# Routed attention and two expert layers on one Trainium2 core: first and last expert swapped, SyncE's order and one queue changed

## The chip, the cores and the metric

The kernel runs on 1 core of a Trainium2 chip. The metric is the device time of one execution in microseconds (us). The engines are TensorE (PE; its weight loads are listed apart as PEld), VectorE (DVE), ScalarE (ACT), GpSimd (POOL) and SyncE (SP), which issues most of the transfers. "Lnnn" is a line of the kernel before.

## The reference, cut to what matters

Three stages follow each other; batch 2, sequence 768.

```python
# 1. attention, 8 heads of 64; only keys of the query's cluster (16 clusters) count
mask = q_assign[:, :, :, None] == k_assign[:, :, None, :]
scores = np.where(mask, scale * q @ k.T, -1e9)
x = softmax(scores) @ v                      # -> x[2, 768, 512]
# 2. one of 8 experts per token
e = fresh_e if (s == 0 or local_gate[b, s] < 0.5) else prev_e
h = np.maximum(x[b, s] @ w1[e], 0.0)         # 512 -> 1024
out[b, s] = p[e] * (h @ w2[e])               # 1024 -> 512
# 3. gated projection, K = 5 taps of a causal convolution
gate = sigmoid(sum(conv_w[k] * shifted(x, k) for k in range(5)))
y = (gate * (x @ w_val)) @ w_out
```

For the inputs that are timed, the experts 0, 1 and 2 get 54, 88 and 118 tokens of the first batch and 88, 65 and 62 of the second; expert 3 gets 170 in all, and the others, by falling number, 289, 228, 211 and 163.

## The kernel before

**Attention.** Sixteen (batch, head) problems are worked as 8 pairs, 12 items of 128 queries each. `prep_steps(g)` prepares a pair while the pair ahead of it is worked. Its steps `stack1` and `stack2` are transfers from SBUF to SBUF; `stack2` (L455) brings the one-hot rows of the clusters into `st`, which PE reads at L668. SyncE issues them in program order with the other loads.

**Routing.** After each half batch, tokens are scattered by expert into `xslots` in HBM by GpSimd, a slot of 428 rows for each of 8 experts and for 3 more: an expert of `HALVED` has a slot for each batch. `keep_rows(gq)` (L513) also copies the rows of a half batch from `xnat` to `xall`; for the last one it is an entry of the list `work`.

**Experts.** They are worked in 8 positions. `AT` gives the expert of the positions 0, 1, 6 and 7; positions 2 to 5 take the experts 4 to 7 in falling order of tokens. `CAPS` is the number of rows worked in each position, `ROWS` the rows of the two batches of a halved expert. The first batch of position 0's expert is worked ahead, in `early_load`, `early_rows` and `early_products`. `do_mm1(k)` is the first product: weights stand, `CAPS[k]` columns of tokens move; experts of `WHOLE` use plain float32 weights (each product two matmul instructions), others split weights (`whi`, `wlo`) and split rows (`xhi`, `xlo`) in three terms. `do_mm2(k)` is the second product: tokens stand, 512 columns of weights move, 24 matmuls for a block of rows; where `FOLD[k]` holds, the last block of 64 rows holds its high and low parts side by side and needs 16, and its two halves are added after (L1206, L1207). Positions 6 and 7 are worked by halves at the end (`do_half`): the first batch of both, then the second batch of both; in between the first batch's rows are loaded back from `x2d` (L1330) for stage 3.

**Rows and weights.** `do_x(k, part)` transposes the rows of a position into one PSUM buffer `xp` (`ps_x` has one) and copies them out; it is called inside `do_mm1(k - 1)`, in two parts for position 2, which has 300 rows. Weights of 1 MB come in through SyncE in the order of `worder`; those to be split go through three staging buffers (`wstg`, `wstg1`, `wstg2`) by `w_stage(at)`, which loads the next pending block into the buffer it is given; after the second half of a split, the buffer just split is given to the next block (L1040). Block 6 is the first staged, block 7 the second.

**Order.** The order of all work is that of the program, on each engine. `tick()` runs inside the products: each tick does one entry of `work` (splits), two of `late`, and one step of `conv` once `XS["ready"]` is set. `conv` is a list of 66 steps that turn the two double-precision matrices of stage 3 into float32 pairs in 8 chunks, over a buffer `wspace` that takes the place of `xnat`: load (L260), four steps on VectorE (`b01` to `b6`), one on ScalarE, three operations on GpSimd (L269, L270, L273), store (L276, L277). What is left of `conv` is done after the first halves (L1324), ahead of the reload.

**End.** Stage 3 ends with `project_out`: ScalarE copies a tile of 128 rows from PSUM to `os_`, a pool of two buffers, and SyncE stores it.

Of the kernel before, what the change touches and what calls it, by code (L numbers as in the profile page):

```python
# [8 lines left out]
F32 = mybir.dt.float32  # L9
# [10 lines left out]
NQT = 6  # L20
NC_ = 16
E = 8
CAPS = (128, 176, 300, 240, 224, 176, 192, 192)
WHOLE = (0, 1, 5, 6, 7)
PACK = 64
AT = {0: 0, 1: 3, E - 2: 2, E - 1: 1}
HALVED = (0, 1, 2)
ROWS = {0: (128, 128), 1: (96, 96), 2: (128, 64)}
V = E + len(HALVED)
NF = len(AT)  # L30
NS = E - NF
SLOT = 428
# [9 lines left out]
def routed_attention_moe_kernel(  # L42
# [12 lines left out]
    nc = tc.nc  # L55
# [8 lines left out]
    xslots = dram.tile([V * SLOT + NCH * 128, XC], F32, name="xslots")  # L64
# [97 lines left out]
    for n, k in enumerate(free):  # L162
        nc.gpsimd.memset(capk[:, :, n], float(CAPS[k]))

# [167 lines left out]
    def w_stage(at):  # L332
        if pending:
            j = pending.pop(0)
            home[j] = at
            wraw[j] = at.tile([128, 2048], F32, tag="w", name="wraw")
            w_load(j, wraw[j])
# [31 lines left out]
    def prep_steps(g):  # L369
        b, p = pairs[g]  # L370
        x = X[g]
        xx = xx_p.tile([128, 4, S], F32R, tag="xx", name="xx")
        st = [st_p.tile([128, 4, S], F32R, tag=f"st{h}", name=f"st{h}") for h in range(2)]
# [80 lines left out]

        def stack2(h):  # L455
            r = o["ohr"].bitcast(F32)
            nc.sync.dma_start(st[h][64:80, 2, :].bitcast(F32), r[32 + 16 * h:48 + 16 * h, :])
            nc.sync.dma_start(st[h][64:80, 3, :].bitcast(F32), r[16 * h:16 * h + 16, :])

        def S0(h, parts=None):  # L460

# [51 lines left out]
    def keep_rows(gq):  # L513
        nc.sync.dma_start(
            xall[384 * gq:384 * gq + 384, :].rearrange("(t p) c -> p t c", p=128), xnat[:, 3 * gq:3 * gq + 3, :]
        )
# [276 lines left out]
    EA = {}  # L793

    def early_load():
        EA["xs"] = xin_p.tile([128, 2, S], F32, tag="x", name="exs")[:, 0, :XC]
        nc.sync.dma_start(EA["xs"], xslots[0:128, :])

    def early_rows():
        xs = EA["xs"]  # L800
# [22 lines left out]
    for i in range(NI):  # L823
        g, qb, t, h = items[i]
# [67 lines left out]
    h_p = mpool("hp", 1)  # L892
    WX = (max(CAPS[0::2]), max(CAPS[1::2]))
    ehh = h_p.tile([128, 8, 2 * WX[1]], F32, tag="h1", name="ehh")[:, :, :128]
# [132 lines left out]
    work = []  # L1027
# [10 lines left out]
    def queue_split(j):  # L1038
        work.append(lambda: w_split(j, 0))
        work.append(lambda: (w_split(j, 1), w_stage(home[j])))  # L1040
# [5 lines left out]
    def tick():  # L1046
# [13 lines left out]
    XT, HT, IDS, PW = {}, {}, {}, {}  # L1060
    NT = [-(-c // 128) for c in CAPS]
    FOLD = [
        ROWS[AT[k]][1] == PACK if k and AT.get(k) in HALVED else 0 < (c - 1) % 128 < PACK and n > 1
        for k, (c, n) in enumerate(zip(CAPS, NT))
    ]
    TR = [
# [1 line left out]
    ]  # L1068
    XS = {}

    def load_x(k):
        if k >= E:
            return
        n, rows = NT[k], TR[k]
        XS[k] = xs_p.tile([128, -(-WX[k % 2] // 128), XC], F32, tag=f"xs{k % 2}", name="xs")
        if k == 0:
            nc.sync.dma_start(XS[k][:, 0, :], xslots[E * SLOT:E * SLOT + 128, :])
            return
        if AT.get(k) in HALVED:
            for t, c in enumerate((AT[k], E + HALVED.index(AT[k]))):  # L1080
                nc.sync.dma_start(XS[k][:TR[k][t], t, :], xslots[c * SLOT:c * SLOT + TR[k][t], :])
            return
        if k in AT:
            src = xslots[AT[k] * SLOT:AT[k] * SLOT + CAPS[k], :]
        else:
            src = xslots[bass.ds(turn[k] * SLOT, CAPS[k]), :]
        if FOLD[k] or k == 0:
            for t, r in enumerate(rows):
                nc.sync.dma_start(XS[k][:r, t, :], src[sum(rows[:t]):sum(rows[:t]) + r, :])
        else:  # L1090
            nc.sync.dma_start(XS[k][:rows[0], :n, :], src.rearrange("(t p) c -> p t c", p=rows[0]))
# [41 lines left out]
    def do_mm1(k):  # L1133
        w = CAPS[k]
        xs = XT.pop(k)
        h = HT[k] = h_p.tile([128, 8, 2 * WX[k % 2]], F32R if k else F32, tag=f"h{k % 2}", name="h")
        c0 = w - PACK if FOLD[k] else w
        for q in range(2):
            if k in WHOLE:
                terms = [(W[k, q].rearrange("p (d f) -> p d f", d=4), xs[0])]  # L1140
            else:
                whv, wlv = [t.rearrange("p (d f) -> p d f", d=4) for t in W[k, q]]
                terms = [(whv, xs[0]), (whv, xs[1]), (wlv, xs[0])]
            for fp in range(2):
                if w > 256:
                    hps = [ps_h.tile([128, 1, 512], F32, tag="h", name="hps") for _ in range(2)]
                else:
                    hps = [ps_h.tile([128, 2, 256], F32, tag="h", name="hps")]
                for fi in range(2):
                    f = 2 * fp + fi  # L1150
                    fs = slice(128 * f, 128 * f + 128)
                    hp = hps[fi][:, 0, :w] if w > 256 else hps[0][:, fi, :w]
                    for n, (a, c) in enumerate(terms):
                        for d in range(4):
                            nc.tensor.matmul(  # L1155
                                hp, a[:, d, fs], c[:, d, :w], start=(n + d == 0), stop=(n + d == len(terms) + 2)
                            )
                m = 2 // len(hps)
                for i, hp in enumerate(hps):
                    fs = slice(4 * q + 2 * fp + m * i, 4 * q + 2 * fp + m * i + m)  # L1160
                    hhi = h[:, fs, c0:c0 + w]
                    nc.scalar.activation(hhi, hp[:, :, :w], AF.Relu)  # L1162
                    for c1, c2, at_ in ((0, c0, 0), (c0, w, c0 + w)):
                        if c1 < c2 and k:
                            nc.vector.scalar_tensor_tensor(  # L1165
                                h[:, fs, at_:at_ + c2 - c1], hp[:, :, c1:c2], 0.0, hhi[:, :, c1:c2].bitcast(F32),
                                op0=ALU.max, op1=ALU.subtract,
                            )
                pops[0] = 2 if (k, q) >= (E - 1, 0) else 1
                tick()  # L1170
                if k < E - 1 and (q, fp) in ((0, 1), (1, 0)):
                    do_x(k + 1, q)
                    if q == 0:
                        load_x(k + 2)
            if k:
                queue_w(wpos[k, q])
        if k == 0:
            queue_split(R + 3)
# [35 lines left out]
    def do_mm2(k):  # L1214
        n = NT[k]
        for t in range(n):
            if t < 2:
                YP[k, t] = ps_y.tile([128, 512], F32, tag="y", name="yp")
            else:
                YP[k, t] = ps_h.tile([128, 512], F32, tag="h", name="yp3")  # L1220
        for q in range(2):
            whv, wlv = mm2_weights(k, q)
            for t in range(n):
                mm2_part(k, t, q, whv, wlv)
                if t < 2:
                    tick()
            if k:
                queue_w(wpos[k, 2 + q])
            else:
                w_stage(stg[q])  # L1230
        HT.pop(k)
        for t in sorted(range(n), key=lambda t: (not FOLD[k] or t < n - 1, t)):
            mm2_out(k, t)

    def do_half(k, t, *apart):
        YP[k, t] = ps_y.tile([128, 512], F32, tag="y", name="yp")
        for q in range(2):
            mm2_part(k, t, q, *mm2_weights(k, q))
            tick()
        mm2_out(k, t, *apart)  # L1240
# [5 lines left out]
    for n, k in enumerate(free):  # L1246
        turn[k] = nc.sync.value_load(ordi[0:1, n:n + 1], min_val=NF, max_val=E - 1)
    w_stage(stg[2])
    queue_split(R + 2)
    ey = ps_y.tile([128, 512], F32, tag="y", name="ey")  # L1250
    for q in range(2):
# [6 lines left out]
    y = y_p.tile([128, 512], F32, tag="y", name="ysb")  # L1258
    nc.scalar.activation(y, ey, AF.Copy, scale=EA["pw"])
    scatter(x2d, EA["ids"], y, 2 * S, "rows of different tokens")  # L1260
    work += [lambda: None, lambda: None, lambda: keep_rows(3)]
    late += overflow_steps()
    do_mm1(0)
    XS["ready"] = True
    do_mm2(0)
    do_mm1(1)
    for k in range(2, E - 1):
        do_mm1(k)
# [7 lines left out]
    with tc.If(nch > 0, preferred_fallthrough_block=False):  # L1276
        with tc.For_i(0, nch, 1) as j:
# [5 lines left out]
            with tc.For_i(0, nd, 1):  # L1283
                for tt in range(12):
                    xs = xs_p.tile([128, 2, XC], F32, tag="xs0", name="xst")
                    nc.sync.dma_start(xs[:, 0, :], xall[128 * tt:128 * tt + 128, :])
                    scatter(xslots, idx1[:, tt:tt + 1], xs[:, 0, :], V * SLOT + NCH * 128)
            if True:
                xs = xs_p.tile([128, 2, XC], F32, tag="xs0", name="xsl")
# [56 lines left out]
    fl = fpool("fl", 2)  # L1346
# [122 lines left out]
    def project_out(b, t, parts=1):  # L1469
        op = OP.pop((b, t))  # L1470
        r0 = S * b + 128 * t
        os_ = fl.tile([128, 512], F32, tag="os", name="os")
        w = 512 // parts
        for n in range(parts):
            cs_ = slice(w * n, w * n + w)
            (nc.vector.tensor_copy if n else nc.scalar.copy)(os_[:, cs_], op[:, cs_])
            (nc.scalar if n else nc.sync).dma_start(out[r0:r0 + 128, cs_], os_[:, cs_])
# [108 lines left out]
```

## Time and profile before

| | us |
|---|---|
| median of the runs | 541.88 (541.17 to 542.16, 3 runs) |
| profiled execution | 539.74 |
| its span, first to last instruction | 538.1 |
| PE busy | 515.7 (96%) |
| DVE busy | 353.1 (66%) |
| ACT busy | 310.0 (58%) |
| POOL busy | 91.3 (17%) |

The mean granted clock of TensorE is 0.990. "Idle before <-X" is the time that an engine stood in front of an instruction and what ended it. The timeline gives start and duration in us, a count if instructions are merged, and the idle time in brackets; SPq and ACTq are transfers issued by SyncE and ScalarE. A matmul's duration includes its pipeline; the spacing of starts is what it costs in a row of them.

### The profile page before, as it was taken

The page shows a single profiled execution, that of the slowest core. Times are in us where ns is not written, and L with a number is a line of the kernel's source. Part 1 is how long each engine was busy: PE and PEld are TensorE (multiplying, and loading weights), DVE is VectorE, ACT ScalarE, POOL GpSimd, SP SyncE. Part 2 cuts the span into 40 slices and gives each one's busy share as a digit, 9 for nine tenths or more (in the row PEclk, how much of TensorE's full clock was granted, in tenths as well). Part 3 has the DMA queues.
Part 4 walks back from the last instruction along what each step waited for, and adds up shares of the span by engine and source line. Part 5 has one row for each costly group of instructions (what it writes and reads, how often), then busy time and mean ns, then how long its engine had stood idle before and what let it go on. Part 6 is the DMA issues. An engine that isn't in the chain of part 4 may idle for free.

```text
span 538.1 us, 8817 instructions
## 1 busy us (share of the span) xinstructions
PE 515.7 (96%) x3189; PEld 409.4 (76%) x3190; DVE 353.1 (66%) x693; ACT 310.0 (58%) x592; POOL 91.3 (17%) x106
## 2 busy tenths in 40 slices
PE   7898999999999999999999499999999999999996
PEld 3775777777677767776956498979889887899885
DVE  5684767575677877655603679986367673599960
ACT  3696868677776778675112355645334463485632
POOL 5011002020203031000310020523421344100000
PEclk9899999999999999999999889999999999999999
DMA  5876787888887866810665866795978855730023
GB/s 146 225 157 212 154 278 198 242 231 207 267 202 272 191 214 135 294 47 2 201 250 193 314 213 222 242 325 194 362 242 314 311 177 203 266 139 2 19 99 117
DMA packets 35524, 108.63 MB, mean 202 GB/s; under 512 B 4718, under 2 KB 5230, under 8 KB 30869
## 3 DMA queue, kind: packets, MB, share of 16 engines
q1 hardware_dynamic: 32341, 101.15, 60.7%
q0 software_dynamic: 2176, 6.31, 3.2%
q10 hardware_dynamic: 960, 0.58, 0.4%
q8 instruction: 26, 0.43, 0.3%
q14 instruction: 21, 0.17, 0.1%
HBM read 58.39 MB, written 29.83 MB: 164 GB/s over the span
## 4 chain that ended last, share of the span: by engine, by line
PE 41%; DMA 5%; SPq 1%; DVE 1%; ACT 1%; issue 1%; ACTq 0%; DVEq 0%
PE hps L1155 13%; PE yp L1195 4%; PE yp L1197 4%; PE yp L1196 4%; PE vp L1421 2%; PE vp L1427 2%; PE vp L1422 2%; PE op L1467 2%; PE op L1466 2%; PE op L1465 2%; DMA xall<-xnat 2%; PE yp L1192 1%; PE yp L1193 1%; DMA wraw<-in_wq_dram 1%; PE xp L1118 1%
## 5 line engine op out<-in xcount | busy, mean ns | idle before, releaser
L675 DVE TENSOR_REDUCE mx<-s 128x1 f32<-128x768 f32 x96 | 91.6, 954 | 59.5 <-PE s L668 53.4
L704 ACT COPY pt<-tp 128x384 f32<-128x384 f32 x148 | 65.7, 483 | 54.4 <-PE tp L699 54.3
L684 ACT ACTIVATE pexp<-s,mx 128x768 f32<-128x768 f32 x96 | 87.1, 907 | 6.7 <-DVE mx L675 4.5
L699 PE MATMUL tp<-ident,pexp 128*128 128x128 f32 x576 | 81.1, 277 | 0.3 <-DVE pt L702 0.2
L699 PEld LDWEIGHTS tp<-ident,pexp 128*128 128x128 f32 x576 | 68.2, 142 | 7.7 <-ACT pt L704 3.3
L366 DVE TENSOR_TENSOR wlo<-wraw,whi 128x1024 fp32r<-128x1024 f32 x40 | 52.9, 1330 | 29.6 <-ACT whi L360 29.6
L711 PE MATMUL pv<-pt,vt 128*64 128x384 f32 x360 | 67.8, 498 | 0.0
L360 ACT CAST whi<-wraw 128x1024 fp32r<-128x1024 f32 x40 | 40.7, 1046 | 31.8 <-DMA wraw<-in_wq_dram 16.8
L664 PE MATMUL s<-st 128*128 128x384 f32 x188 | 57.3, 386 | 1.5 <-ACT pexp L684 1.5
L1155 PE MATMUL hps<-xhi,wone 128*128 128x192 f32 (+2 forms) x320 | 50.7, 318 | 0.0
L668 PE MATMUL s<-st 80*128 80x384 f32 x188 | 49.0, 342 | 1.4 <-DMA st<-ohr 1.4
L1155 PEld LDWEIGHTS hps<-xhi,wone 128*128 128x128 f32 x320 | 49.0, 195 | 1.6 <-ACT xhi L1124 0.6
L664 PEld LDWEIGHTS s<-st 128*128 128x128 f32 x188 | 28.6, 191 | 17.8 <-issue 7.3
L711 PEld LDWEIGHTS pv<-pt,vt 128*64 128x64 f32 x360 | 21.9, 136 | 23.8 <-issue 23.8
L1162 ACT ACTIVATE h<-hps 128x352 fp32r<-128x352 f32 (+5 forms) x36 | 16.9, 474 | 33.8 <-PE hps L1155 33.7
L1195 PE MATMUL yp<-whi,h 128*112 128x512 f32 (+4 forms) x88 | 35.0, 397 | 0.8 <-ACT h L1162 0.8
L668 PEld LDWEIGHTS s<-st 80*128 80x128 f32 x188 | 34.4, 190 | 1.7 <-issue 1.7
L1197 PE MATMUL yp<-whi,h 128*112 128x512 f32 (+4 forms) x88 | 34.7, 394 | 0.0
L1196 PE MATMUL yp<-wlo,h 128*112 128x512 f32 (+4 forms) x88 | 34.7, 394 | 0.0
L384 POOL TENSOR_TENSOR xx<-xkq,xx 128x768 fp32r<-128x768 f32 x8 | 14.6, 1822 | 117.5 <-ACT xx L378 117.5
L1407 DVE SCALAR_TENSOR_TENSOR gt<-xf,convw_sb,gt 128x768 f32<-128x768 f32 x32 | 32.0, 1015 | 0.4
L1165 DVE SCALAR_TENSOR_TENSOR h<-hps,h 128x128 fp32r<-128x128 f32 (+7 forms) x52 | 18.4, 391 | 16.7 <-ACT h L1162 15.1
(280 smaller groups left out, 893.0 us busy)
## 6 DMA issues: line engine op xcount, KB each, us to landing
wraw<-in_wq_dram SPq DMA_DIRECT2D x20, 1024.0 KB
st<-xx SPq DMA_DIRECT2D x48, 384.0 KB
wone<-in_wq_dram SPq DMA_DIRECT2D x12, 1024.0 KB
xslots<-padrow SPq DMA_DIRECT2D x15, 771.0 KB
xkq<-in_kq_dram SPq DMA_DIRECT2D x15, 384.0 KB
wspace<-in_wd_dram SPq DMA_DIRECT2D x8, 512.0 KB
xall<-xnat SPq DMA_DIRECT2D x4, 771.0 KB
vt<-in_v_dram SPq DMA_DIRECT2D x8, 384.0 KB
```

Of the source, the lines that this page charges most:

```text
L366: nc.vector.tensor_tensor(lo[:, c], t[:, c], hi[:, c].bitcast(F32), op=ALU.subtract)
L664: nc.tensor.matmul(ps[:, n, :384], st[:, 1, q0:q0 + 128], st[:, 0, 384 * n:384 * n + 384], start=True, stop=False)
L668: nc.tensor.matmul(ps[:, n, :384], st[0:80, 2, q0:q0 + 128], st[0:80, 3, 384 * n:384 * n + 384], start=False, stop=True)
L675: nc.vector.tensor_reduce(mx, ps[:, :, :384], axis=AX.XY, op=ALU.max, negate=True)
L684: nc.scalar.activation(pt, ps[:, :, :384], AF.Exp, bias=mx[:, 0:1], accum_out=Zt[i // 6][:, t, h:h + 1])
L699: nc.tensor.transpose(tp[:, k, :], p[:, 128 * kt:128 * kt + 128], ident)
L704: nc.scalar.copy(dst, tp)
L711: nc.tensor.matmul(PVs[u][64 * h:64 * h + 64, :], Vt[g][:, kt, h, :], PT[u, h][:, kt, :], start=(kt == 0), stop=(kt == NQT - 1), skip_grou ...
L1155: nc.tensor.matmul(hp, a[:, d, fs], c[:, d, :w], start=(n + d == 0), stop=(n + d == len(terms) + 2))
L1195: nc.tensor.matmul(yp[:r], h[:, fa, hi], whv[:, f, :], start=(q == 0 and f == 0), stop=False)
L1196: nc.tensor.matmul(yp[:r], h[:, fa, hi], wlv[:, f, :], start=False, stop=False)
L1197: nc.tensor.matmul(yp[:r], h[:, fa, lo], whv[:, f, :], start=False, stop=(q == 1 and f == 3))
```

## The change

Experts 0 and 1 change places: expert 1 goes to position 0, with 72 rows of the second batch there, expert 0 to position 7 with 64 and 96 rows, of which the block of 64 (the first batch) is folded; position 6 works 184 rows for 192. `halves` and the first line of `do_half` let the folded block be either batch. The last `keep_rows` leaves the list `work` and stands right behind the first `w_stage`; two empty entries keep their place, and `XS["ready"]` is set after the second product of position 0. `stack2` of the second pair goes to ScalarE's queue. `os_` gets four buffers.

```diff
-CAPS = (128, 176, 300, 240, 224, 176, 192, 192)
+CAPS = (72, 176, 300, 240, 224, 176, 184, 160)
-AT = {0: 0, 1: 3, E - 2: 2, E - 1: 1}
+AT = {0: 1, 1: 3, E - 2: 2, E - 1: 0}
-ROWS = {0: (128, 128), 1: (96, 96), 2: (128, 64)}
+ROWS = {1: (128, 72), 2: (120, 64), 0: (64, 96)}
...
         def stack2(h):
             r = o["ohr"].bitcast(F32)
-            nc.sync.dma_start(st[h][64:80, 2, :].bitcast(F32), r[32 + 16 * h:48 + 16 * h, :])
-            nc.sync.dma_start(st[h][64:80, 3, :].bitcast(F32), r[16 * h:16 * h + 16, :])
+            q = nc.scalar if g == 1 else nc.sync
+            q.dma_start(st[h][64:80, 2, :].bitcast(F32), r[32 + 16 * h:48 + 16 * h, :])
+            q.dma_start(st[h][64:80, 3, :].bitcast(F32), r[16 * h:16 * h + 16, :])
...
-        nc.sync.dma_start(EA["xs"], xslots[0:128, :])
+        nc.sync.dma_start(EA["xs"], xslots[AT[0] * SLOT:AT[0] * SLOT + 128, :])
...
-        ROWS[AT[k]][1] == PACK if k and AT.get(k) in HALVED else 0 < (c - 1) % 128 < PACK and n > 1
+        PACK in ROWS[AT[k]] if k and AT.get(k) in HALVED else 0 < (c - 1) % 128 < PACK and n > 1
...
+    def halves(k):
+        cols = AT[k], E + HALVED.index(AT[k])
+        return cols[::-1] if ROWS[AT[k]][0] == PACK else cols
...
-            nc.sync.dma_start(XS[k][:, 0, :], xslots[E * SLOT:E * SLOT + 128, :])
+            c = E + HALVED.index(AT[0])
+            nc.sync.dma_start(XS[k][:CAPS[0], 0, :], xslots[c * SLOT:c * SLOT + CAPS[0], :])
...
-            for t, c in enumerate((AT[k], E + HALVED.index(AT[k]))):
+            for t, c in enumerate(halves(k)):
...
-    def do_half(k, t, *apart):
+    def do_half(k, b, *apart):
+        t = b ^ (ROWS[AT[k]][0] == PACK)
...
     w_stage(stg[2])
+    keep_rows(3)
+    work += [lambda: None, lambda: None]
     queue_split(R + 2)
...
-    work += [lambda: None, lambda: None, lambda: keep_rows(3)]
     late += overflow_steps()
     do_mm1(0)
+    do_mm2(0)
     XS["ready"] = True
-    do_mm2(0)
     do_mm1(1)
...
-        os_ = fl.tile([128, 512], F32, tag="os", name="os")
+        os_ = fl.tile([128, 512], F32, tag="os", name="os", bufs=4)
```

## Rows read from the trace of the kernel before

**Rows 1.** What PE waited for over the whole span: us in total, times, longest.

```profile
PE xp L1118 <- DVE xlo L1129: 6.9, 1, 6.9
...
PE s L668 <- DMA st<-ohr: 1.4, 1, 1.4
```

**Rows 2.** Timeline of PE, positions 0 and 1.

```profile
278.18 3.74 PE L1155 MATMUL hps<-xhi,wone 128*128 128x128 f32 x32
...
293.36 4.94 PE L1155 MATMUL hps<-xhi,wone 128*128 128x176 f32 x32
...
308.54 1.45 PE L1118 MATMUL xp<-ident,xs 128*128 128x128 f32 x6 [6.85 <-DVE xlo L1129]
...
313.87 0.83 PE L1155 MATMUL hps<-xhi,whi 128*128 128x300 f32 x4
```

**Rows 3.** Timeline of VectorE in position 1.

```profile
298.94 1.22 DVE L366 TENSOR_TENSOR wlo<-wraw,whi 128x1024 fp32r<-128x1024 f32 x1
...
304.58 0.43 DVE L230 TENSOR_SCALAR wspace<-wspace 128x512 int32<-128x512 int32 x1 [4.14 <-DMA wspace<-in_wd_dram]
...
307.72 0.76 DVE L1129 TENSOR_TENSOR xlo<-xp,xhi 128x600 fp32r<-128x600 f32 x1
```

**Rows 4.** Timeline of SyncE's queue, positions 0 and 1.

```profile
279.24 11.41 SPq L326 DMA_DIRECT2D wraw<-in_wq_dram  x2
...
292.68 0.58 SPq L514 DMA_DIRECT2D xall<-xnat  x1
301.00 0.36 SPq L260 DMA_DIRECT2D wspace<-in_wd_dram  x1
```

**Rows 5.** Timeline of ScalarE, first split of block 7.

```profile
295.71 1.05 ACT L360 CAST whi<-wraw 128x1024 fp32r<-128x1024 f32 x1 [5.81 <-DMA wraw<-in_wq_dram]
```

**Rows 6.** Stretches: PE, PEld, DVE, ACT, POOL busy, PE clock, DMA share, GB/s.

```profile
288.00:294.00 6.00, 6.00 (x18) 3.02 (x18) 4.07 (x22) 1.90 (x5) 0.00 (x0) 1.00 0.38 142
...
308.50:311.00 2.50, 2.46 (x10) 2.08 (x11) 2.46 (x6) 0.66 (x1) 0.00 (x0) 0.50 1.01 419
```

**Rows 7.** The chain that ended last, first products: start, us, work (224, 176, 192 columns).

```profile
364.01 5.36 PE hps L1155 x48
...
386.83 4.78 PE hps L1155 x32
...
428.87 10.41 PE hps L1155 x64
```

**Rows 8.** Timeline of PE, start of the halves and of stage 3.

```profile
440.08 0.47 PE L1195 MATMUL yp<-whi,h 128*128 128x512 f32 x1 [0.81 <-ACT h L1162]
...
460.55 1.47 PE L1377 MATMUL x2p<-ident,x2nat 128*128 128x128 f32 x12
```

**Rows 9.** Timeline of VectorE, the folded output of half (6, 1).

```profile
456.57 0.74 DVE L1207 SCALAR_TENSOR_TENSOR ysb<-part,pw,ysb 64x512 f32<-64x512 f32 x1 [8.08 <-ACT part L1206]
```

**Rows 10.** Timeline of GpSimd in the first halves.

```profile
448.98 1.29 POOL L269 TENSOR_TENSOR wspace<-wspace 128x512 f32<-128x512 f32 x1 [1.06 <-ACT wspace L265]
...
451.59 1.29 POOL L273 TENSOR_TENSOR wspace<-wspace 128x512 fp32r<-128x512 f32 x1
453.04 0.95 POOL L635 DMA_INDIRECT x2d<-ysb,ids  x1 [0.16 <-issue]
```

**Rows 11.** Timeline of SyncE's queue, the reload.

```profile
456.04 9.41 SPq L1330 DMA_DIRECT2D x2nat<-x2d  x5
```

**Rows 12.** Timeline of ScalarE, last two output tiles.

```profile
533.37 1.06 ACT L1476 COPY os<-op 128x512 f32<-128x512 f32 x2 [1.46 <-DMA out_dram<-os]
```

**Rows 13.** Timeline of PE, its last matmul.

```profile
532.86 0.39 PE L1467 MATMUL op<-whi,gl 128*128 128x512 f32 x1
```

**Rows 14.** Timeline of ScalarE: an issue at the start, an exp of the first pair.

```profile
2.10 0.62 ACTq L171 DMA_DIRECT2D cw<-in_convw_dram  x1
...
36.01 0.90 ACT L684 ACTIVATE pexp<-s,mx 128x768 f32<-128x768 f32 x1
```

**Rows 15.** Timeline of PE, scores of the first pair.

```profile
37.93 0.59 PE L664 MATMUL s<-st 128*128 128x384 f32 x2
```

## Prediction

> **What bounds the kernel now.** I read the list of what TensorE (PE) waited for first. In 538.1 us it has one long wait, 6.9 us for VectorE's `xlo`; the longest single one after it is the 1.4 us for `st<-ohr` [rows 1]. So a change is worth what it takes from that stall, from PE's instructions, or from the tail where PE is done.
>
> PE's timeline shows where the stall is. The first product of position 1 starts at 293.36; after three quarters of it PE needs its one transpose buffer `xp` for the second part of position 2's rows and gets it 6.85 us late, at 308.54; position 2 starts at 313.87 [rows 2]. VectorE's timeline shows why: it sat 4.14 us until `wspace`, the first double-precision chunk, landed at 304.5, converted a piece, and only then did `xlo` (from 307.72), which frees `xp` [rows 3]. SyncE's timeline shows why the chunk was late: it reuses the buffer `xnat`, whose copy (L514) went out at 292.68, so L260 could go only at 301.00, and every load behind it on this queue with it [rows 4]. So the order of issue, not bandwidth, makes this stall. In 308.5 to 311 PE's granted clock is 0.50 (the 1.2 of 1.2 and 2.4 GHz): the stall cost a slow restart too [rows 6].
>
> **The change, part by part.**
>
> *SyncE's new order.* Two moves. `keep_rows(3)` goes right behind the first staged load (279.24), and the conversion starts two ticks later, in position 1. The copy took at most 8.3 us, with block 7 and position 2's rows queued ahead of it [rows 4]; issued near 280 it is over by about 289, in front of the second staged load, which goes out near 290.3 as before; were it not, each us late there would shift the rest by a us.
>
> The missing `None`s move something else. Both halves of the split of staged block 7 now fall in position 0's second product, and the second half calls `w_stage`: block 9 goes into that same buffer and waits until VectorE has done the split, and SyncE waits with it. Behind it stand block 10 (1 MB), the first chunk (0.5 MB), the second, and position 3's rows. Block 7 is on ScalarE from 295.71 [rows 5]; its two halves there take 1.05 each, VectorE's low parts 1.2 each behind, with two small steps between: VectorE is done about 299.7 (it began this half at 298.94 before [rows 3]). Block 9 then goes out at 299.7 and moves data from about 301 (301.00 to 304.5 for an unqueued half megabyte [rows 3, 4] is some 2.2 us of latency and 1.3 of transfer at 419 GB/s [rows 6], part of the latency behind the last byte). Blocks 9 and 10 and the chunk are 2.6 MB: 6.3 us at 419 GB/s. The chunk is there at about 308, later than the 304.5 of before.
>
> VectorE meets that wait in another place, though: one tick pair later, behind `xlo` part 0 and in front of part 1. Part 0: VectorE is free at 299.7, has two pairs of `h` steps, six small steps and the 0.76 of `xlo`: done about 303.0. PE, which wants `xp` at 301.5 (293.36 + 32 x 0.149 + 0.9 of transposes + 16 x 0.149, spacing from [rows 7]), stands 1.5 us. Then 0.8 of transposes and 16 matmuls: position 2 starts at 306.2 and after 0.6 needs `xlo` part 1. That is the chunk (308.0), 1.1 of conversion, 0.7 of `xlo`: 309.85, a second stall of 3.1 us. Position 2 effectively starts at 309.85 - 0.6 = 309.3, against 313.87 [rows 2]: **4.6 us gained**, if neither short stall lowers the clock. Bounds: nothing of it, if the chunk comes 4.6 later; 7.7, if it is no later than before, since 306.2 is then PE's own start.
>
> After that the conversion stays two ticks late. VectorE comes to position 2 earlier by as much as PE does, with the same work ahead, so I add nothing for it; the price is at the end (below).
>
> *Swapped experts: columns.* In the chain 64 matmuls of 192 columns take 10.41 (0.163 each) and 32 of 176 take 4.78 (0.149): 0.83 ns a column [rows 7]. Position 6 loses 8 columns, position 7 loses 32, 64 matmuls each: 0.43 + 1.70 = **2.1 us**. PE is unbroken there, so it counts. Position 0 loses 56 columns, 128 to 72. By the same slope that would be 64 x 56 x 0.83 ns = 3.0 us; but 48 matmuls of 224 one-pass columns took 5.36, 0.112 each [rows 7], no less than a matmul of 128 two-pass columns (3.74 for 32, at most 0.117 [rows 2]), where one pass at half of 0.83 ns a column would give 0.093. The near rows thus show a floor near 0.112, and I take 0; bounds 0 and 3.0. Either way it isn't on the path: the stall behind it ends with a DMA. The Trainium skill (TensorE: Matmul & The Clock Gate, section "LDWEIGHTS (loading the stationary operand)") speaks against this edit: a weight load takes the number of its columns over 1.2 ns, 107 ns for 128, however few columns follow. By it, as an estimate, position 0 would save at most 64 x 5 ns = 0.3 us; the rows of 224 columns agree, no run here has 72. The smaller load of position 0's rows and its transposes are hidden the same way.
>
> *Swapped experts: the second product of position 7.* Its 64-row half is now folded: 16 matmuls for 24, 8 x 0.233 = 1.9 us off PE (88 matmuls took the 20.47 from 440.08 to 460.55 [rows 8]). The last halves are bound by the reload, though. Before: PE started them at 440.08, the reload (L1330) went out at 456.04, PE used it at 460.55 without a recorded wait [rows 1, 8, 11]. The conversion now has two more steps left: its three GpSimd operations (448.98 to 452.9) stood ahead of the scatter of half (7, 0) (453.04) [rows 10]; now they stand behind it, and the last store and the reload behind them on SyncE. Counted from the start of the halves: 40 matmuls, +9.3; a folded output needs 2.4 from PE's end to VectorE's end (half (6, 1): 64 matmuls give 455.0, VectorE ends at 457.3 [rows 9]), +11.8; scatter 1.0; three operations 3.9, +16.9; store and reload, +17.4 (before: +16.0). PE is done at +18.6 instead of +20.5, but its first three tiles are 0.79 MB: 1.9 us at 419 GB/s and 2.2 of latency after the issue, +21.5, and the third's transposes end near +22.1 (before: +21.9). The 1.9 is lost, and I take **-0.2**; bounds +1.9 and, with a reload 1.3 later still, -1.5.
>
> *Output staging, 4 buffers.* Near the end ScalarE stood 1.46 us for `out_dram<-os`, that is for a buffer, and copied the last two tiles from 533.37 one behind the other [rows 12]. PE's last matmul ends at 532.86 + 0.39 = 533.25 [rows 13]. With four buffers tile 4 is copied before that and the last copy starts near 533.4 instead of 534.05: **0.65 us**; bounds 0 and 0.8.
>
> *Second pair's one-hot rows from ScalarE.* SyncE sends them behind the pair's six `stack1` transfers, and PE waits 1.4 us [rows 1]. On ScalarE four issues stand between the rows and the exp of 36.01; such an issue took 0.62 [rows 14], together 2.5. That exp frees the buffer of the scores that PE starts at 37.93 [rows 15]; it would end near 39.4, so PE stands 1.5 there and has lost about what it gains. I take 0; bounds +1.4 (issues hidden) and -1.1 (2.5 less 1.4).
>
> *Sum.* 4.6 + 2.1 - 0.2 + 0.65 + 0 = 7.2 us. The profiled execution took 539.74 us (span 538.1 and 1.6 around it): 532.5. Its time is 2.1 below the median of the timed runs, 541.88, and taken from that the forecast is 534.7 us.
>
> **Rivals.**
>
> *Both stalls go* (the chunk lands by 305, or the reload isn't late). For it: SyncE is no longer blocked for 7 us by L260. Against it: 2 MB stand ahead of the chunk. Worth up to 3.1 + 1.5 more, and 1.9 of the fold: about 530.
>
> *The clock falls in the new stalls.* Before, six transposes and 16 matmuls after the stall took 313.87 - 308.54 = 5.3 instead of 3.2 us. For it: two stalls close together. Against it: each is less than half of 6.85. Price 2.1, with a somewhat later chunk 4: 537 to 539.
>
> *The chunk is late enough to undo it.* Blocks 9 and 10 now stand in front of it and SyncE waits on VectorE for them. At the 142 GB/s of 288 to 294 [rows 6] the 2.6 MB take 18 us: the chunk lands near 319, PE resumes near 321, and the time is about 546. It decides from a landing at 315.2, 7.2 later than forecast: then all gains are spent. Against it: that stretch had little queued.
>
> *The change does nothing measurable*: a landing of about 315, or stalls that reappear as waits for weights: 541 to 543.
>
> **How the numbers follow.** Within 0.2% (1.1 us) is what a measurement here can't tell from none. Chances: the forecast (531 to 536.8) 0.50; both stalls gone 0.13; clock or partly late chunk 0.20; nothing measurable 0.07; late chunk, slower, 0.10. Faster 0.83, same 0.07, slower 0.10. The range runs from the full removal (530) to the lower gain of the clock case (539.5).
>
> **What would show it.** Right: L514 near 280; L260 behind two loads near 300; a PE wait for `xlo` of some 3 us near 306 to 310 and a shorter one before it; position 2's first matmul by 309; position 7 at 0.136 us a matmul; position 0 still at 0.11; a new PE wait for the reload of 1 to 3 us; no ScalarE wait for `out_dram<-os`; L668's wait replaced by one of L664 for the exp. Wrong: if the 6.9 us wait is whole, if position 0 speeds up, or if weights are waited for after 320.

## The result and the profile after

The changed kernel takes 548.46 us (546.68 to 551.63, 5 runs) against 541.37 for the kernel before in the same session: a ratio of 1.014 (95%: 1.0113 to 1.0167). It is slower by 7 us where 7 less were forecast. Its profiled execution, 551.63 us, is the slowest of its five, so differences read from its trace (span 549.9 against 538.1) are larger than those of the medians. Line numbers from here on are those of the kernel named.

First the list of what PE waited for, changed kernel: the line waited at, the releaser, total, times, longest.

```profile
PE x2p L1385 <- DMA x2nat<-x2d: 7.4, 2, 5.7
PE tp L700 <- ACT pt L705: 4.4, 1, 4.4
PE hps L1161 <- DVE xlo L1135: 3.8, 1, 3.8
PE xp L1124 <- DVE xlo L1135: 2.9, 1, 2.9
```

The 6.9 and the 1.4 us of [rows 1] are gone, and four waits, 18.5 us together, stand in their place. Two are the forecast ones at position 2 (`xp`, `hps`); the other two are in attention and at the reload.

Attention: timelines of ScalarE, then PE, changed kernel.

```profile
37.49 0.58 ACTq L458 DMA_DIRECT2D st<-ohr  x1
38.11 1.97 ACTq L459 DMA_DIRECT2D st<-ohr  x1
40.12 1.94 ACTq L458 DMA_DIRECT2D st<-ohr  x1
42.10 0.97 ACTq L459 DMA_DIRECT2D st<-ohr  x1
43.44 0.48 ACT L705 COPY pt<-tp 128x384 f32<-128x384 f32 x1 [5.98 <-issue]
```

```profile
39.05 0.49 PE L700 MATMUL tp<-ident,pexp 128*128 128x128 f32 x3
43.98 0.90 PE L700 MATMUL tp<-ident,pexp 128*128 128x128 f32 x3 [4.43 <-ACT pt L705]
```

The four issues hold ScalarE for 5.5 us. The copy of `pt` behind them frees PE's buffer, so PE stands 4.4, and then runs slowly (a stretch: PE, PEld, DVE, ACT, POOL busy, granted clock, DMA share, GB/s):

```profile
46.00:52.00 6.00, 6.00 (x27) 3.55 (x26) 2.00 (x4) 2.79 (x6) 0.00 (x0) 0.61 0.89 316
```

Position 0 starts at 285.52 instead of 278.18 [rows 2]:

```profile
285.52 3.69 PE L1161 MATMUL hps<-xhi,wone 128*128 128x72 f32 x32
```

SyncE's queue around the positions 0 and 1, then VectorE, then PE at position 2, changed kernel.

```profile
287.05 0.35 SPq L326 DMA_DIRECT2D wraw<-in_wq_dram  x1
287.50 0.41 SPq L515 DMA_DIRECT2D xall<-xnat  x1
...
299.75 0.36 SPq L326 DMA_DIRECT2D wraw<-in_wq_dram  x1
...
309.45 1.25 SPq L260 DMA_DIRECT2D wspace<-in_wd_dram  x2
```

```profile
317.64 0.43 DVE L230 TENSOR_SCALAR wspace<-wspace 128x512 int32<-128x512 int32 x1 [4.21 <-DMA wspace<-in_wd_dram]
...
318.71 0.77 DVE L1135 TENSOR_TENSOR xlo<-xp,xhi 128x600 fp32r<-128x600 f32 x1
```

```profile
311.45 0.89 PE L1124 MATMUL xp<-ident,xs 128*128 128x128 f32 x6 [2.85 <-DVE xlo L1135]
...
319.54 0.55 PE L1161 MATMUL hps<-xlo,whi 128*128 128x300 f32 x2 [3.78 <-DVE xlo L1135]
```

The copy (L515) goes out early, as forecast, and the one long stall is now two. Less the 7.34 us of attention, the first chunk is there at 310.3 and position 2 resumes at 312.2, against 308.0 and 309.85 in the prediction. The lateness begins with the first staged weights (ScalarE's first split of block 6, kernel before, then changed kernel):

```profile
286.72 1.05 ACT L360 CAST whi<-wraw 128x1024 fp32r<-128x1024 f32 x1 [6.17 <-DMA wraw<-in_wq_dram]
```

```profile
295.88 1.04 ACT L360 CAST whi<-wraw 128x1024 fp32r<-128x1024 f32 x1 [3.64 <-DMA wraw<-in_wq_dram]
```

They land 8.5 us after the start of position 0 before, and 10.4 after: the copy now goes out right behind them. From the issue of this load to its split it takes 7.5 to 8.2 us in the seven kernels of this study with SyncE's old order, and 8.7 to 11.7 in the eleven with the new one (e10, where the rows go out later, 9.9).

The halves and the reload: SyncE's queue, GpSimd, PE, changed kernel.

```profile
450.47 0.53 SPq L345 DMA_DIRECT2D wlo<-wld  x1
459.78 0.33 SPq L276 DMA_DIRECT2D whd<-wspace  x1
...
460.78 0.39 SPq L276 DMA_DIRECT2D whd<-wspace  x1
463.55 0.32 SPq L277 DMA_DIRECT2D wld<-wspace  x1
466.01 3.05 SPq L1338 DMA_DIRECT2D x2nat<-x2d  x5
```

```profile
449.07 2.16 POOL L273 TENSOR_TENSOR wspace<-wspace 128x512 fp32r<-128x512 f32 x1
...
458.32 0.92 POOL L636 DMA_INDIRECT x2d<-ysb,ids  x1 [5.00 <-DVE ysb L1213]
...
461.89 1.63 POOL L273 TENSOR_TENSOR wspace<-wspace 128x512 fp32r<-128x512 f32 x1
```

```profile
444.48 0.46 PE L1201 MATMUL yp<-whi,h 128*120 128x512 f32 x1 [0.82 <-ACT wspace L265]
...
468.99 1.09 PE L1385 MATMUL x2p<-ident,x2nat 128*128 128x128 f32 x4 [5.71 <-DMA x2nat<-x2d]
471.74 1.97 PE L1385 MATMUL x2p<-ident,x2nat 128*128 128x128 f32 x8 [1.66 <-DMA x2nat<-x2d]
```

The halves start at 444.48, and the reload leaves 21.5 us later, against 16.0 before [rows 8, 11]. SyncE sends nothing from 450.5 to 459.8, though GpSimd had been done since 451.2 with the chunk that it stores then. But the reload does not wait for that: the last chunk's three operations stand behind the scatter of half (7, 0), GpSimd ends its low part at 463.5, and the reload goes out when the store of this part has landed (from the chain that ended last):

```profile
463.55 2.33 DMA wld<-wspace
```

The scatter itself is late. PE was done with half (7, 0) near 453.8 (40 matmuls of 0.233 us from 444.48), but on ScalarE a step of the last chunk stood ahead of the half's output, and waited for VectorE:

```profile
454.93 0.63 ACT L265 ACTIVATE wspace<-wspace 128x512 f32<-128x512 int32 x1 [3.95 <-DVE wspace L237]
...
455.98 0.68 ACT L1209 ACTIVATE ysb<-yp,pw 64x512 f32<-64x512 f32 x1
```

The clock from the reload on, 1.00 before:

```profile
465.00:470.00 5.00, 1.01 (x4) 0.72 (x4) 0.00 (x0) 0.00 (x0) 1.00 (x3) 0.71 0.78 217
470.00:475.00 5.00, 2.66 (x11) 2.19 (x11) 2.02 (x3) 1.75 (x3) 0.00 (x0) 0.50 1.05 400
```

End: ScalarE's copies, changed kernel.

```profile
540.62 3.32 ACT L1484 COPY os<-op 128x512 f32<-128x512 f32 x5 [6.51 <-issue]
```

No wait for `out_dram<-os` is left [rows 12].

### The profile page after: what moved, and what is told of

It is laid out like the page before. It is cut to its first block, busy times and chain, and to the rows that moved or that the text cites. A ratio compares the mean times of both kernels' runs of the same rounds, so it can differ in the third digit from the quotient of the medians.

```text
span 549.9 us, 8792 instructions
## 1 busy us (share of the span) xinstructions
PE 518.0 (94%) x3181; PEld 409.4 (74%) x3182; DVE 356.2 (65%) x700; ACT 309.5 (56%) x593; POOL 96.1 (17%) x106
## 5 line engine op out<-in xcount | busy, mean ns | idle before, releaser
L700 PE MATMUL tp<-ident,pexp 128*128 128x128 f32 x576 | 82.3, 279 | 4.6 <-ACT pt L705 4.4
L366 DVE TENSOR_TENSOR wlo<-wraw,whi 128x1024 fp32r<-128x1024 f32 x40 | 55.8, 1407 | 25.6 <-ACT whi L360 25.4
L712 PE MATMUL pv<-pt,vt 128*64 128x384 f32 x360 | 69.1, 507 | 0.0
L1161 PE MATMUL hps<-xhi,wone 128*128 128x176 f32 (+3 forms) x320 | 47.0, 305 | 0.0
L1161 PEld LDWEIGHTS hps<-xhi,wone 128*128 128x128 f32 x320 | 45.4, 190 | 1.6 <-issue 0.5
L1168 ACT ACTIVATE h<-hps 128x352 fp32r<-128x352 f32 (+6 forms) x36 | 16.2, 453 | 38.6 <-PE hps L1161 38.4
L1201 PE MATMUL yp<-whi,h 128*112 128x512 f32 (+4 forms) x80 | 31.8, 397 | 0.8 <-ACT wspace L265 0.8
L1203 PE MATMUL yp<-whi,h 128*112 128x512 f32 (+4 forms) x80 | 31.5, 394 | 0.0
L1202 PE MATMUL yp<-wlo,h 128*112 128x512 f32 (+4 forms) x80 | 31.5, 394 | 0.0
L636 POOL DMA_INDIRECT xslots<-xnat,idx x12 | 12.0, 1003 | 93.3 <-DVE red L627 69.7
```

The lines of the kernel that those rows point to most:

```text
L366: nc.vector.tensor_tensor(lo[:, c], t[:, c], hi[:, c].bitcast(F32), op=ALU.subtract)
L700: nc.tensor.transpose(tp[:, k, :], p[:, 128 * kt:128 * kt + 128], ident)
L712: nc.tensor.matmul(PVs[u][64 * h:64 * h + 64, :], Vt[g][:, kt, h, :], PT[u, h][:, kt, :], start=(kt == 0), stop=(kt == NQT - 1), skip_grou ...
L1161: nc.tensor.matmul(hp, a[:, d, fs], c[:, d, :w], start=(n + d == 0), stop=(n + d == len(terms) + 2))
L1201: nc.tensor.matmul(yp[:r], h[:, fa, hi], whv[:, f, :], start=(q == 0 and f == 0), stop=False)
L1202: nc.tensor.matmul(yp[:r], h[:, fa, hi], wlv[:, f, :], start=False, stop=False)
```

## The experiments

One table serves all. The columns are PE's milestones, from the timelines: P0, the first product of position 0 (us from the start); then the lengths of four stretches: P0 to position 1's second product (Y1), Y1 to the halves (H), H to the first product of stage 3 (`vp`, V), V to the end of PE's last matmul. Then the median time and the ratio to the kernel before in its session. The stretches come from one profiled execution each, up to 3.4 us away from its kernel's median (e8).

| kernel | P0 | P0-Y1 | Y1-H | H-V | V-end | median | ratio |
|---|---|---|---|---|---|---|---|
| before | 278.2 | 49.96 | 111.94 | 22.90 | 70.27 | 540.2 to 541.6 | |
| after | 285.5 | 48.96 | 110.00 | 29.91 | 71.59 | 548.46 | 1.014 |
| e1_sync | 277.6 | 47.64 | 110.03 | 30.81 | 72.22 | 543.64 | 1.0053 (1.0034 to 1.0072) |
| e2_only_act | 284.8 | 49.75 | 111.94 | 23.04 | 70.25 | 545.62 | 1.0087 (1.0065 to 1.011) |
| e3_catch_up | 277.5 | 48.46 | 110.03 | 28.74 | 72.06 | 543.55 | 1.006 (1.0039 to 1.008) |
| e4_loads_first | 278.3 | 48.38 | 110.09 | 27.48 | 72.09 | 543.17 | 1.0052 (1.0036 to 1.0068) |
| e5_wlast_behind | 277.4 | 48.77 | 110.01 | 24.58 | 72.52 | 540.93 | 1.0018 (1.0001 to 1.0035) |
| e6_swap_os | 277.4 | 51.50 | 110.02 | 25.54 | 72.14 | 542.88 | 1.0063 (1.0041 to 1.0084) |
| e7_order_only | 278.7 | 47.12 | 111.94 | 27.02 | 72.12 | 543.85 | 1.0082 (1.0054 to 1.011) |
| e8_all_conv | 276.8 | 47.70 | 110.00 | 28.43 | 71.78 | 544.22 | 1.009 (1.007 to 1.011) |
| e9_last_on_dve | 278.3 | 50.31 | 110.03 | 27.10 | 72.34 | 542.22 | 0.9999 (0.9982 to 1.0016) |
| e10_nones_behind | 279.1 | 49.56 | 111.95 | 26.87 | 71.67 | 545.26 | 1.0052 (1.0036 to 1.0068) |
| e11_pool_queue | 279.0 | 50.03 | 111.95 | 22.89 | 70.27 | 540.57 | 0.9986 (0.9969 to 1.0003) |
| e12_before_dve | 278.9 | 50.51 | 111.94 | 22.90 | 70.27 | 541.39 | 0.9994 (0.998 to 1.0007) |
| e13_whi_early | 277.6 | 49.80 | 110.03 | 21.86 | 76.27 | 540.52 | 1.0009 (0.9991 to 1.0026) |
| e14_whi_early_pool | 277.7 | 47.93 | 110.02 | 21.92 | 75.31 | 539.81 | 0.9999 (0.9984 to 1.0013) |
| e15_pool_os | 276.8 | 49.90 | 111.94 | 22.89 | 70.27 | 538.45 | 0.9967 (0.9954 to 0.998) |
| e16_os_only | 278.6 | 50.83 | 111.93 | 22.89 | 70.27 | 539.07 | 0.9982 (0.9969 to 0.9994) |

In its profile the changed kernel's span is some 12 us longer: 7.3 up to P0, 7.0 in H-V and 1.3 in V-end are lost, 1.0 up to Y1, 1.9 in Y1-H and 0.8 behind PE's end are gained.

**The queue of the one-hot rows.** `e1_sync` is the changed kernel with the rows back on SyncE, `e2_only_act` the kernel before with that edit alone, `e11_pool_queue` the kernel before with GpSimd's queue:

```diff
-            q = nc.scalar if g == 1 else nc.sync   # the changed kernel
+            q = nc.sync                            # e1
+            q = nc.gpsimd if g == 1 else nc.sync   # e11, for nc.sync in the kernel before
```

> The changed kernel with the second pair's one-hot rows sent by SyncE again. Theory A (ScalarE is held by its four issues for 6 us, and PE with it): all of the 7.3 us by which the first product began later comes back, 548.5 - 7.3 = 541.2 us, PE's 4.4 us wait for ScalarE's copy is gone and the 1.4 us wait for the rows is there again. Rival (the transfers are slow from any queue, and the loss is mostly a low clock that has another cause): 2 us or less come back, 546 to 548.

> The kernel before with that one edit alone. Theory A: 541.4 + 7.3 = 548.7 us, with issues of about 2 us on ScalarE. Rival (the loss needs the rest of the change): within 1.1 us of before, as the prediction had it.

> Kernel before, with the second pair's one-hot rows sent by GpSimd's queue in place of SyncE's (GpSimd has nothing to do from 31 to 51 us). Theory: in the kernel with ScalarE's queue it wasn't the transfers' place that cost, but ScalarE, held by four issues for 5.6 us while exp and copies waited behind them; held there, GpSimd delays nobody: 540.3 us, at best 1 less (539.3 to 541). Rival: the rows ahead of SyncE's own transfers, or a slower start of GpSimd's transfers, cost PE the time: 543 to 546 us.

e1 and e2 came out between the two expectations, and they add up: 0.53% and 0.87% make the 1.4% of the whole. So ScalarE's queue costs 4.7 us of the time (3.5 to 6.0; 6.6 at P0 in e2's profile), and the rest of the change loses 2.9 by itself. e11 came out as expected. On GpSimd the four issues are short, and nobody waits behind them (its timeline in e11):

```profile
37.70 0.75 POOL L458 DMA_DIRECT2D st<-ohr  x1 [5.88 <-ACT ohr L445]
38.45 0.51 POOL L459 DMA_DIRECT2D st<-ohr  x1
38.96 0.49 POOL L458 DMA_DIRECT2D st<-ohr  x1
39.44 0.49 POOL L459 DMA_DIRECT2D st<-ohr  x1
```

So it was not the transfers leaving SyncE's queue that cost, but ScalarE's time.

**Swap and order apart.** `e6_swap_os` undoes SyncE's order (and the queue) in the changed kernel, `e7_order_only` makes it in the kernel before:

```diff
+    keep_rows(3)
+    work += [lambda: None, lambda: None]
     queue_split(R + 2)
...
-    work += [lambda: None, lambda: None, lambda: keep_rows(3)]
...
+    do_mm2(0)
     XS["ready"] = True
-    do_mm2(0)
```

> Kernel before with the swapped experts and the four output buffers alone; SyncE's order and the one-hot rows' queue as before. C: no step of the conversion is later than before, so the columns give about 2 us, the four output buffers 0.7 to 0.9, and 80 in place of 88 matmuls of 0.23 us in the halves 1.9 us, of which the reload takes back 0.5 to 1: 537.7 us (536.5 to 539). Rival: the folded half that now comes first among position 7's halves makes the reload late by itself: 540 to 542 us.

> Kernel before with SyncE's new order alone. C: position 1 ends about 2 us earlier than before, counted from the start of position 0, but the conversion ends about three steps later and the reload loses 4 to 6 us: 544 us (543 to 546). Rival: the late reload comes of the swap, and the order alone gains 1 to 2.5 us: 539 to 540.5 us.

e7 came out as expected; e6 missed by 5 us and lies above its rival too. The third stretch shows the gain of the columns, 1.92 us in every kernel with the swap. The second shows that of the order: 2.84 us in e7, but one profile is not enough here. The nine kernels that have the order as the change makes it lie between 47.12 and 50.31, mean 48.5, the seven without it between 49.75 and 51.50, mean 50.4, so the order is worth 1.8 on the mean. The fourth and fifth stretch show the losses. H-V is 22.9 to 23.0 and V-end 70.3 in every kernel that has neither the swap nor the order. With either one TensorE waits for the reload and the clock falls. In H-V the two losses add up and more (2.6 in e6, 4.1 in e7, 7.9 in e1); the slow clock of V-end is paid once (1.9, 1.9, 2.0), and e1 has both gains, so it loses no more than e6 or e7 by itself.

What holds the reload is not the same everywhere. In e1 and e7 it is what it is in the changed kernel, the low part's store (landed at 456.6 and 457.8, the reload out 0.1 later). In e6 the conversion is not late; there SyncE sends `wlo` at 445.88, waits at the overflow branch until it has landed (452.83), and only then sends the last store (453.74).

**Conversion caught up.** e1 with two more steps of `conv`, ahead of position 7 (e3) or between position 0's two products (e4).

```diff
+    for _ in range(2):
+        conv.pop(0)()
     do_mm1(E - 1)
```

> As e1, and two steps of the conversion are done ahead of position 7's first product, so that its end lies where it lay before; nothing else is moved. Theory B (the reload is late because the last conversion steps and their store stand ahead of it): PE's waits for the reload (7.4 us) go, with the slow restart: 541.2 - 6.6 = 534.6 us (533.5 to 536.5). Rival (the folded output and its scatter are late by themselves): 540 to 541.5.

> As e1, and the first two loads of the conversion go out behind position 0's first product, ahead of the staged blocks 8 to 10; the conversion is thereby two steps ahead, and its end is where it was before, as in e3. Theory C (the second stall for xlo is the chunk queued behind the blocks 9 and 10): that 3.8 us stall and its slow restart go, xlo part 1 is not late, and the time is 3 to 4 us below e3: 530.5 to 532. Rival (VectorE is late with its own work, the chunk hides behind it): as e3, 534 to 535.

Both missed, on both theories: the conversion's steps stood where they stand in the kernel before, and the reload was late all the same. In e4 the second stall did go (no wait at `hps`), but the first grew to 6.2 us from e3's 3.7, and P0-Y1 is as long as in e3 (PE, e4):

```profile
PE xp L1124 <- DVE xlo L1135: 6.2, 1, 6.2
```

In e3 GpSimd was done with the last chunk at 450.25, yet the store of its high part left at 453.75. What SyncE waited for (e3):

```profile
SPq L1286 <- SPq L1286: 6.4, 2, 3.3
```

L1286 is the overflow branch: SyncE waits there until what it has sent has landed, and `whi` and `wlo`, 1 MB each, stand just ahead of it (sent at 443.18 and 443.55, landed at 449.74 and 452.84). With the conversion on time, as in e3 and e6, this wait holds the reload; in the changed kernel, where the last low part came later still, it did not.

**Out of the branch's way, and quicker.** e5 is e3 with `w_last(0)` behind the branch; e8 has three steps caught up; e9 is e5 with the last chunk's three GpSimd operations on VectorE; e12 does that alone in the kernel before.

```diff
-    w_last(0)
     nch = nc.values_load(infoi[0:1, 0:1], min_val=0, max_val=NCH)
...
+    w_last(0)
     do_half(E - 2, 0)
...
+            eng = nc.vector if (n, c) == (1, 3) else nc.gpsimd     # e9, e12
```

> Second form of the theory (C): the reload is late because SyncE, before it can pass the overflow branch, waits until the weights whi and wlo that it issued just ahead of it have landed (449.74 and 452.84 us in the catch-up kernel, issues at 443.18 and 443.55), and only then sends the last store, whose data stood ready at 446.4 and 450.25. With the two loads moved behind the branch the store leaves at about 446.5, its low part at 450.3, the reload at about 454 (18 us after the halves start in place of 21.7), and the wait of the first x2p transposes falls from 5.8 to about 2 us: 540 us (539 to 541.5). Rival (D): the time of the reload is set by the traffic and not by the place where SyncE waits; the same bytes move, only later: 543 to 544.5 us.

> As the kernel with the two loads behind the branch, and with three steps of the conversion, not two, ahead of the last position. C: the last store is out before the halves, the reload waits only for the first halves' rows (about 15 us after the halves start, against 21.7 in the catch-up kernel), and the transposes start with the end of the halves or at most 1 us behind; the clock doesn't fall there: 537.5 us (536 to 539). D: 541 to 543.5 us, since the two weight loads then run beside the reload.

> As the kernel with two steps caught up and the two weight loads behind the branch, and the last chunk's three GpSimd operations (446.01 to 450.46 there) on VectorE, which stood idle. Theory: the reload hangs on the chain of the last chunk (GpSimd's low part, store, its landing, then the reload), and PE's clock halves after the stall and costs about as much again. The low part is then ready near 448.5, the reload leaves near 452 and lands its first tile near 455, as PE ends the halves (455.0): no wait above 0.5 us, granted clock 1.00 from 455 to 470, and of the 540.9 us of that kernel some 3.5 go: 537.3 us (536 to 538.7). Rival: what binds the reload is the traffic of the two weights and the rows, so it moves by under 1 us, or the clock falls without the stall: 539.5 to 541 us.

> Kernel before with the last chunk's three GpSimd operations on VectorE alone. Theory: there the reload is in time (no wait of the x2p transposes, clock 1.00), so an earlier reload is worth nothing: 540.3 us, within 1. Rival: the end of the conversion holds more than the reload: 538 to 539 us.

e5 did what was expected, with 2.9 us of `x2p` wait left, 1.7 the longest. But the clock fell with these short waits too:

```profile
460.00:465.00 5.00, 4.33 (x14) 4.21 (x14) 3.13 (x4) 0.58 (x1) 0.00 (x0) 0.50 0.46 146
```

e8 missed: the extra step put the last block's split behind it on VectorE, PE waited 1.3 us for `wlo` in the first half, and the stores were no earlier. e9 missed by 5 us and lies above its rival too: its low part was done at 450.65, but the high part's store landed 8.2 us after its issue, behind the weights (SyncE, e9):

```profile
SPq L1341 <- DMA whd<-wspace: 6.3, 1, 6.3
```

e12 gave nothing, as expected. So the chain of instructions that makes the last chunk holds the reload in the changed kernel, but shortening it is not enough: behind it stand the branch, and then the landing of the stores.

**Where the bytes stand.** e13 is e9 with `whi` early, as in the kernel before, and `wlo` behind the first reload; e14 has GpSimd's queue as well.

```diff
-    w_last(0)
+    last_part(0, 0)     # whi, into the staging buffer that is free first
...
     first = [reload(nc.sync, 0, 1), reload(nc.sync, 1, 3), reload(nc.sync, 3, 6)]
+    last_part(0, 1)     # wlo
```

> As the kernel with the last chunk on VectorE, but with the weight load split: whi goes into the staging buffer that is free first and stands ahead of the overflow branch, wlo goes out behind the first reload. In the kernel with the last chunk on VectorE the low part was ready at 450.65 and the store out at 450.68, yet the reload left at 458.43, since the store of the high part, sent at 449.13 behind the 2 MB of whi and wlo (445.85, 446.23), landed only at 457.3. Traffic theory: without the 2 MB ahead of them the stores land within 2.5 to 3.5 us, the reload leaves 14 to 16 us after the halves start (19.8 there), the x2p wait is under 1 us and the clock stays at 1.00 there: 537.5 us, ratio 0.992 to 0.997 to the kernel before. Rival: the reload waits for the first halves' rows in x2d, or the transposes now wait no longer but the vp products wait for wlo: ratio 0.998 to 1.003.

> The same, with the second pair's one-hot rows on GpSimd's queue (0.9986 of the kernel before there). Traffic theory: 537 us, ratio 0.990 to 0.996. Rival: 0.997 to 1.002.

The traffic theory held for the reload: the first store landed 2.4 us after its issue, the reload left 15.5 us after the halves started, `x2p` waited 0.8. The rival held for the time: `vp` waits for the weights that were put back (PE, e13).

```profile
457.45 1.09 PE L1391 MATMUL x2p<-ident,x2nat 128*128 128x128 f32 x8 [0.80 <-DMA x2nat<-x2d]
459.27 0.45 PE L1435 MATMUL vp<-xh,whi 128*128 128x384 f32 x1 [0.72 <-ACT xh L1395]
463.43 0.69 PE L1436 MATMUL vp<-xh,wlo 128*128 128x384 f32 x1 [3.71 <-DMA wlo<-wld]
```

The queue has 2 MB of weights, the last stores and 0.79 MB of rows to move between the halves and `vp`, and in the orders tried one of them is late whichever comes first. e14 came out the same way, on its rival. That the stretch can't be shorter under any order wasn't shown.

**The empty entries.** They do not keep their place, as "The change" has it: they stood behind the split of block 6, and the changed kernel has them ahead of it. e10 is e7 with the two behind the split.

> SyncE's order alone, with the two empty steps behind the split of staged block 6 and not ahead of it, which is how the prediction had read the change. Theory: the split of block 6 is two ticks earlier, the load of the next block and the chunk behind it go out 1.5 to 2.5 us earlier, the second stall of position 2 (2.2 us in the order-alone kernel) shrinks to under 1 us; the reload is as late as there. 542.3 us (541.3 to 543.3). Rival: the chunk's landing is set by the queue's bytes, not by the split: 543.5 to 544.3 us.

Missed, though its ratio is no worse than e7's: the weights to be split aren't there any earlier, so nothing behind them moves up; the second stall was 4.0 us, and PE lost 2.5 in position 0, since the split, two ticks earlier in ScalarE's program, now holds it ahead of the `h` that PE needs (ScalarE, e10):

```profile
290.21 1.04 ACT L360 CAST whi<-wraw 128x1024 fp32r<-128x1024 f32 x1 [8.72 <-DMA wraw<-in_wq_dram]
```

**The tail, and a faster version.** The kernel before with four `os_` buffers, alone (e16) and with GpSimd's queue (e15):

> Kernel before with four output buffers alone. Prediction's term: 0.65 us, ratio 0.9988 (0.9975 to 1). Rival: nothing, 0.9995 to 1.0005; from 0.9995 upward the term is void, between the two the run can't tell.

> Kernel before with the second pair's one-hot rows on GpSimd's queue and four output buffers, nothing else: the two terms add, 0.8 and 0.7 to 0.9 us: ratio 0.997 (0.9955 to 0.9985). Rival: the output buffers give nothing, as the sender of the last tiles ends the kernel and not the copies: 0.9986.

Both came out as expected: e16 gains 1.0 us and e15, the fastest kernel of the study, 1.8. With V-end as before, e16's gain stands behind PE's end, 4.8 us of span before and 4.0 in e16.

## Why the prediction was wrong

**ScalarE's queue: the first step that failed.** Predicted 0, bounds +1.4 and -1.1; measured -4.7 us. The four issues were priced at 0.62 each, from an issue at the kernel's start [rows 14], when the DMA engines had hardly begun (busy share 0.05 up to 2 us, 0.45 from 2 to 3). Near 40 us they took 5.5 together (why an issue takes longer there was not tested), and the trace of before had the price for these very transfers, on SyncE:

```profile
37.67 1.94 SPq L457 DMA_DIRECT2D st<-ohr  x1
39.65 1.68 SPq L458 DMA_DIRECT2D st<-ohr  x1
41.37 0.59 SPq L457 DMA_DIRECT2D st<-ohr  x1
42.00 0.59 SPq L458 DMA_DIRECT2D st<-ohr  x1
```

The sum named the exp as the work behind them; the `pt` copy came first, and PE's slow restart (granted clock 0.61 from 46 to 52) came on top.

**The reload: the second.** Predicted -0.2, worst case -1.5. In the changed kernel H-V grew by 7.0 us and V-end by 1.3. The chain that the step summed (folded output, scatter, three GpSimd operations, store, reload) is the one that held the reload; its terms were too small. The low part ended 19.0 us after the halves started, not 16.9: the sum counted the last chunk's operations on GpSimd as late, but its steps on VectorE and ScalarE were late too and stood ahead of the folded output. From there to the reload the sum took 0.5 us and the store took 2.3 to land (2.5 in all; the kernel before has 3.2, from 452.9 to 456.04 [rows 10, 11]). The third tile was there 5.7 us after the reload went out, not 4.1. And the clock, which fell there for 10 us, was given to position 2 alone; in V-end it costs 1.3 to 2.3 (table, without e13 and e14). The sum also lacked what would have been next: SyncE's wait at the branch (9.3 us between `wlo` and the first store) and the 2 MB of weights ahead of the stores, which e3 to e9 brought to light.

**SyncE's order: right in kind, too large.** 4.6 us predicted; 1.8 up to Y1 on the mean of the kernels with it (1.0 in the changed kernel's profile, 2.84 in e7's). The two short stalls came where the prediction put them, longer than it had them (2.9 and 3.8 for 1.5 and 3.1). The step said that the early copy would be over before the second staged load. Instead it slowed the first load, so the second went out at 292.4 (299.75 less 7.34) and not at 290.3, and the chunk landed 2.3 later than forecast. How much it slows the first load varies: the two slowest of the nine, 11.7 us in e9 and 11.1 in e13, have the two longest P0-Y1. The empty entries, which the prediction had put behind the split of block 6, stand ahead of it; e10, no nearer to the forecast, shows that this wasn't the cause. The order's price, "two ticks late", then came due at the reload.

**Columns: right.** 2.1 predicted, 1.92 measured. Position 0's 32 matmuls took 3.69 us with 72 columns and 3.74 with 128: nothing, as said.

**Tail: right.** 0.65 predicted, 1.0 measured (0.3 to 1.7), 0.8 behind PE's end in e16's profile.

**Rivals.** "The clock falls in the new stalls" was the nearest, but its price of 2.1 was for one place, and the clock fell at three (attention, position 2, the reload). The slower rival, a late chunk, had the right sign for a wrong reason: the chunk landed well ahead of 315.2.

## What to carry to other kernels

Price an issue where it will stand, from issues of the same stretch with the queue as full as there, and then name the first instruction behind it on its engine. Where a stretch ends with a transfer, sum the queue's bytes ahead of it and the places where the issuing engine waits for landings, not only the chain of instructions that makes the data. When one cause of the wait is taken away, ask what ends last then. A gain that arrives at such a point early is spent there, and waits of 3 us in all cost about 2 more in clock here (e5, e7).

## What the hardware showed

- The same four transfers of 48 KB took 5.5 us to issue on ScalarE, 4.8 on SyncE and 2.2 on GpSimd, with the DMA engines' busy share at 1.02, 0.84 and 0.98 meanwhile; each held its engine.
- With waits for the reload of 1.7 to 5.7 us (the longest of each kernel), PE's granted clock stood at 0.50 (1.2 GHz) from 459.0 to 465.8 us in e5 and from 467.1 to 477.3 in the changed kernel. In e13, where PE stood 0.8 and then 3.7, it was 0.61 from 460 to 465.
- The last chunk's first store, 256 KB, landed 6.1 us after its issue in e5 and 8.2 in e9, with the 2 MB of weights sent 3 us ahead of it both times; what makes the difference was not settled. In e13, where `whi` had landed before and `wlo` came after, it landed after 2.4.
- One 1 MB load on SyncE, with the copy of 771 KB right behind it, took 8.7 to 11.7 us from issue to first use, against 7.5 to 8.2 without.
